# Sigmoid attention and a two-layer MLP on one core: moving operands set 16 floats apart from the weights, and no matmul wider than 448 columns

## Chip, cores and metric

The kernel runs on one core of a Trainium2 chip. The metric is the device time of one execution in microseconds (us); three runs of the kernel before gave 1015.92, 1016.38 and 1016.88 us, with a median of 1016.38 us.

## What is computed

Attention with a sigmoid in place of the softmax, over 8 batches of 12 heads with 448 positions and 64 columns, feeds an MLP of 768 to 2048 to 768 columns over 3584 tokens. All inputs are float32.

```python
scores = scale * np.matmul(q, k.transpose(0, 1, 3, 2)) - np.log(S)
attn = 1.0 / (1.0 + np.exp(-scores))
x = np.matmul(attn, v)                       # then (B*S, 768)
h = x @ w_in
g = h * (1.0 / (1.0 + np.exp(-1.702 * h)))
out = g @ w_out
```

## The kernel before

The program has two stages on TensorE. The first (to about 250 us) is attention: the 48 pairs of heads are taken two at a time, and for each group TensorE runs a burst of score matmuls and then a burst of value matmuls. The second (from 250 us to the end) is the MLP. It is computed by a bilinear scheme with 26 products in place of 32 blocks: weights, x and g are first added up into sums on VectorE, each product is a set of matmuls, and the results are added into the outputs. 104 products of 36 matmuls each make 3744 matmuls.

Precision is kept by splitting. A float32 operand is rounded to the fast float32r form and the rest is kept in a second tile; each product of two operands is three matmuls (hi by hi, hi by rest, rest by hi). `split_pair` (line 628) does this for q and k of a pair of heads into the tile `qk`; `pair_of` (line 1048) does it for x and g into the tile `pair`; `split_piece` (line 827) for the weights into the two ring tiles of the tag `raw64`.

Each matmul has a weight load of its own: 128 columns of the stationary operand (`lhsT`) are loaded, then up to 512 columns of the moving operand (`rhs`) stream past. In the MLP the weights (`w`) are stationary and x or g moves, at line 869. In the scores k is stationary and q moves, at line 673, two matmuls side by side on the two halves of the rows. Both have 448 moving columns of float32r.

Where the operands lie in a partition: every tile of the pools `sb` and `att` has a length that is a multiple of 64 floats (3072 for the weights ring, 1536 for a sum, 3584 for a pair, 1792 for `qk`, 896 for the raw loads and for `a`), and within a tile the slices that a matmul reads begin at multiples of 64 too (448 is 7 times 64, and weights are cut at multiples of 128). So at line 869 and line 673 the stationary and the moving operand begin at the same place, counted mod 64 floats.

The order of all work is worked out ahead by the planner `Plan.run` from fixed costs (line 41 has MM = 0.203 us for a matmul), and each engine runs its list in that order. The change doesn't touch a cost or a task.

`Mlp.products` (line 1091) hands a width to the first matmul of a product that begins a new PSUM accumulator: `self.widths` at line 894, chosen by how many products have passed since the last such one. It replaces the 448 columns of that matmul by 468 to 484. The columns past 448 fall into the unused end of the 512-column PSUM bank, and nothing reads them.

Of the kernel before, what the change touches and what calls it, by code (L numbers as in the profile page):

```python
# [8 lines left out]
F32 = mybir.dt.float32  # L9
F32R = mybir.dt.float32r  # L10
# [9 lines left out]
P = 128  # L20
T = 448
ROWS = 4

PACE, LEAD = 2.9, 1
SOON, PATIENCE, CROWDED, LATE = 4, 0.3, (1, 5), 6.0
# [3 lines left out]
    qk=3, vraw=2, a=6, al=2, raw64=2, e=4, qkraw=5, x32=2,  # L29
# [373 lines left out]
def sigmoid_attention_mlp(ctx: ExitStack, tc: tile.TileContext, qk, v, w, out):  # L403
    nc = tc.nc
    B, HD, S2 = qk.shape
# [3 lines left out]
    S = S2 // 2  # L409
# [15 lines left out]
    sb = ctx.enter_context(tc.tile_pool(name="sb", bufs=2))  # L425
    dram = ctx.enter_context(tc.tile_pool(name="dram", bufs=1, space=bass.MemoryType.DRAM))

    spaces, psum = {}, {}
# [24 lines left out]
    ps = spaces["q0"].tile([P, 512], F32, tag="q0_0", name="still", bufs=1)  # L453
# [149 lines left out]
    def load_pair(b, p):  # L603
# [21 lines left out]
            t_q[0].landing = t_v.landing = LATE if (b, p) <= CROWDED else 3.3  # L625
        return t_q, qkr, t_v, vr

    def split_pair(b, p, t_q, qkr):
        if (b, p) == (0, 0):
            return t_q[0], qkr  # L630
        s = buffer("qk")
        make_s = lambda: make(s, "qk", [P, 2, S2], F32R, f"qk{b}_{p}")
        if (b, p) == (0, 1):
            ts = []
            for t, cols, costs in zip(t_q, (slice(0, S + P), slice(S + P, S2)), ((None, 0.42, 0.72), (None, 0.25, 0.41))):
                ts.append(round_and_rest(
                    costs, s, lambda cols=cols: qkr.tile[:, cols], [t], [qkr],
                    lambda cols=cols: s.tile[:, 0, cols], lambda cols=cols: s.tile[:, 1, cols],
                    lambda: None if s.tile is not None else make_s(),
                ))  # L640
            return ts, s
        t = round_and_rest(
            (0.94, 0.63, 1.09), s, lambda: qkr.tile, t_q, [qkr],
            lambda: s.tile[:, 0], lambda: s.tile[:, 1], make_s,
        )
        return [t], s

# [15 lines left out]
    def scores(n, c, t_s, s, place):  # L663
        ps, a = two_banks(place), buffer("a")

        terms = ((0, 1), (1, 0), (0, 0)) if n else ((0, 0),)

        def emit():
            make(ps, ps.tag, [P, 2, 512], F32, f"sc{n}_{c}")
            src = [s.tile[:, 0], s.tile[:, 1]] if n else [s.tile]  # L670
            for i, (kk, qq) in enumerate(terms):
                for j, rows in enumerate(halves_of_rows):
                    nc.tensor.matmul(  # L673
                        ps.tile[:, j, :S], lhsT=src[kk][rows, S + c * P : S + (c + 1) * P], rhs=src[qq][rows, :S],
                        start=i == 0, stop=i == len(terms) - 1,
                    )

        t = task("PE", (0.8 if not c and n % 2 == 0 else 0.605) if n else (1.2, 1.4, 0.8)[c], emit, t_s, [ps, s])
        return t, sigmoid(f"a{n}_{c}", a, ps, t), a
# [207 lines left out]
    class Mlp:  # L887


        def __init__(self, sequence, before):  # L890
            self.sequence, self.before = sequence, before
            self.w = [Sums(W_SUMS[0], W_USES, w_leaf(m), dve(PIECE), combine, fresh(f"ws{m}", PIECE, "s"),
                           KEEP_FOR[f"w{m}"], self.put_w(m)) for m in range(2)]
            self.gap, self.widths = 1, (0, 472, 484, 476, 468, 472)
            self.saved, self.recent = {}, [(None, None)]
            self.way = self.ways()
            self.x = [Sums(X_SUMS[0], X_USES, self.x_leaf(q), dve(XB), combine, fresh(f"xs{q}", XB, "s"),
                           KEEP_FOR[f"x{q}"], self.put_x(q)) for q in range(2)]
            self.g_nodes = [{}, {}]
            self.g = [Sums(G_SUMS[0], G_USES, self.g_leaf(q), dve(GB), combine, fresh(f"gs{q}", GB, "g"),  # L900
                           KEEP_FOR[f"g{q}"], self.put_g(q)) for q in range(2)]
            self.last_pair = {}
            self.units, self.turn = [], None
            self.nets = {}
            self.products_of = [(q, m, r) for q, m, r in sequence if q < 2]
            for m in range(2):
                for v in W_USES:
                    self.w[m].left[v] -= 1
            for i, (q, m, r) in enumerate(sequence):
                if self.way[i] == "made":  # L910
                    self.w[m].left[W_USES[r]] += 1
                    self.w[m].need(W_USES[r], i)
                if q < 2:
                    (self.x, self.g)[m][q].need((X_USES, G_USES)[m][r], i)
            for q in range(2):
                self.nets[q, 0] = Net(self, q, 0, *H_SUMS, X_SUMS[1], GB, 4, "h", self.gelu)
                self.nets[q, 1] = Net(self, q, 1, *O_SUMS, G_SUMS[1], XB, NJ, "o", self.store)
            self.spilled_g = {}
# [23 lines left out]
        def x_leaf(self, q):  # L942
            def leaf(v):
                k, n = divmod(v, ROWS)
                b = plan.slot()
# [102 lines left out]
        def pair_of(self, q, m, v, n, name, sign):  # L1048
            key = (name, v, sign)
            sums = (self.x, self.g)[m][q]  # L1050
            if key in self.last_pair:
                sums.left[v] -= 1
                sums.used(v)
                return self.last_pair[key]
            node = sums.get(v)
            sums.left[v] -= 1
            b = buffer("pair")
            w = n // T

            def part(d):  # L1060
                return lambda: b.tile[:, d, :w]

            def first():
                make(b, "pair", [P, 2, 4, T], F32R, name)

            if sign > 0:
                t_hi = on_either((act(n), lambda: nc.scalar.copy(part(0)(), node.view())),  # L1067
                                 (cast(n), lambda: nc.vector.tensor_copy(part(0)(), node.view())),
                                 node.done, [b, node.b], first)
            else:  # L1070
                def negative():
                    first()
                    nc.scalar.mul(part(0)(), node.view(), -1.0)

                t_hi = task("ACT", act(n), negative, node.done, [b, node.b])

            def rest():
                if sign > 0:
                    nc.vector.tensor_tensor(part(1)(), node.view(), part(0)().bitcast(F32), op=ALU.subtract)  # L1079
                else:  # L1080
                    nc.vector.scalar_tensor_tensor(
                        part(1)(), node.view(), -1.0, part(0)().bitcast(F32), op0=ALU.mult, op1=ALU.subtract)

            t_lo = task("DVE", dve(n), rest, [t_hi], [b, node.b])
            node.readers += [t_hi, t_lo]
            sums.used(v)
            self.last_pair.clear()
            self.last_pair[key] = t_lo, b
            return t_lo, b
# [253 lines left out]
```

## Time and profile before

| | us |
|---|---|
| median of three runs | 1016.38 |
| span of the profiled execution, first to last instruction | 1014.2 |
| TensorE busy in it | 1009.7 |
| VectorE busy in it | 939.6 |
| ScalarE busy in it | 609.1 |

The profile page gives a span of 1014.2 us for the profiled execution; no whole time of that execution is listed apart. The median of the runs is 2.2 us above the span, which is taken as what lies around it. Busy time is the union of an engine's instructions. Matmuls are pipelined: one lasts about 366 ns from its start to its end, but the next begins some 203 ns after it. So the pace is read from the starts of many matmuls in a row, and not from the mean duration.

### The profile page before, as it was taken

What the parts mean: (1) busy time and instruction counts of PE and PEld (TensorE: products, weight loads), DVE (VectorE), ACT (ScalarE), POOL (GpSimd) and SP (SyncE); (2) the same over time, 40 slices, a digit from 0 to 9 for tenths busy, and PEclk for the clock granted to TensorE, in tenths of its full rate; (3) what the DMA queues carried; (4) which work ended last, traced back from release to release, by engine and by line L of the source; (5) the groups of instructions that cost most, each with busy time, mean ns of one, the idle gap of its engine ahead of it and who ended that gap; (6) DMA issues with size and microseconds to landing.
All of it is one profiled execution on the core that took longest, in us unless ns stands there. A gap on an engine that the chain in (4) does not pass through costs nothing.

```text
span 1014.2 us, 13730 instructions
## 1 busy us (share of the span) xinstructions
PE 1009.7 (100%) x5587; PEld 836.4 (82%) x5587; DVE 939.6 (93%) x658; ACT 609.1 (60%) x489; POOL 0.2 (0%) x4
## 2 busy tenths in 40 slices
PE   9999999999999999999999999999999999999998
PEld 5545555555999999999999999999999999999997
DVE  6987888898899999898999899999999999999996
ACT  7978887895345566356365447675554646344643
POOL 0000000000000000000000000000000000000000
PEclk9999999999999999999999999999999999999999
DMA  9999899777995799968869978996667782889546
GB/s 359 399 384 341 312 383 344 292 257 274 377 365 225 296 346 380 399 253 341 332 242 322 366 275 295 374 393 269 249 244 269 291 324 78 321 327 352 198 151 245
DMA packets 62222, 310.42 MB, mean 306 GB/s; under 512 B 6480, under 2 KB 14928, under 8 KB 58192
## 3 DMA queue, kind: packets, MB, share of 16 engines
q1 hardware_dynamic: 62160, 309.55, 80.6%
q8 instruction: 44, 0.72, 0.3%
q14 instruction: 18, 0.15, 0.0%
HBM read 198.80 MB, written 110.72 MB: 305 GB/s over the span
## 4 chain that ended last, share of the span: by engine, by line
PE 100%; ACT 0%; issue 0%
PE p L869 75%; PE av L704 11%; PE sc L673 9%; PE sc L689 2%; PE av L717 2%; PE still L455 0%; ACT o L1145 0%
## 5 line engine op out<-in xcount | busy, mean ns | idle before, releaser
L869 PE MATMUL p<-gp,w 128*128 128x448 f32 (+2 forms) x1872 | 380.7, 366 | 0.0
L869 PE MATMUL p<-xp,w 128*128 128x448 f32 (+1 forms) x1872 | 380.6, 366 | 0.0
L869 PEld LDWEIGHTS p<-xp,w 128*128 128x128 f32 x1872 | 351.9, 188 | 28.6 <-issue 0.7
L869 PEld LDWEIGHTS p<-gp,w 128*128 128x128 f32 x1872 | 351.9, 188 | 28.2 <-issue 0.2
L659 ACT ACTIVATE a<-sc,bias 128x896 f32<-128x896 f32 x168 | 156.3, 1020 | 37.6 <-PE sc L689 27.5
L1258 ACT COPY h<-p 128x1792 f32<-128x1792 f32 x41 | 67.6, 1658 | 98.0 <-PE p L869 83.7
L704 PE MATMUL av<-a,vraw 128*64 128x448 f32 x576 | 113.5, 543 | 0.1
L1258 ACT COPY o<-p 128x1344 f32<-128x1344 f32 x42 | 53.7, 1283 | 98.8 <-PE p L869 91.2
L673 PEld LDWEIGHTS sc<-qk 64*128 64x128 f32 x846 | 77.1, 185 | 23.7 <-PE sc L689 15.5
L673 PE MATMUL sc<-qk 64*128 64x448 f32 x846 | 92.8, 369 | 0.0
L704 PEld LDWEIGHTS av<-a,vraw 128*64 128x64 f32 x576 | 39.2, 137 | 63.5 <-issue 44.6
L1292 DVE TENSOR_TENSOR h<-h,h 128x1792 f32<-128x1792 f32 x45 | 90.4, 2020 | 0.2
L532 DVE TENSOR_TENSOR qk<-qkraw,qk 128x896 fp32r<-128x896 f32 (+2 forms) x48 | 51.5, 1078 | 3.3 <-ACT qk L526 2.6
L1118 ACT ACTIVATE h<-h 128x1792 f32<-128x1792 f32 x27 | 45.8, 1702 | 11.4 <-DVE h L1292 11.4
L1067 ACT CAST gp<-kg 128x1792 fp32r<-128x1792 f32 x20 | 33.9, 1696 | 28.0 <-DVE kg L810 13.4
L1292 DVE TENSOR_TENSOR o<-o,o 128x1344 f32<-128x1344 f32 x31 | 47.7, 1552 | 0.1
L1079 DVE TENSOR_TENSOR xp<-x,xp 128x1344 fp32r<-128x1344 f32 x28 | 43.5, 1552 | 1.0 <-ACT xp L1067 1.0
L1079 DVE TENSOR_TENSOR gp<-kg,gp 128x1792 fp32r<-128x1792 f32 x21 | 42.4, 2019 | 1.4 <-ACT gp L1067 1.4
L835 DVE TENSOR_TENSOR w<-ws,w 128x1536 fp32r<-128x1536 f32 x23 | 40.3, 1753 | 3.1 <-ACT w L832 2.9
L734 DVE COPY x<-av 128x896 f32<-128x896 f32 x17 | 18.6, 1094 | 23.8 <-PE av L717 23.8
L832 ACT CAST w<-ws 128x1536 fp32r<-128x1536 f32 x17 | 25.2, 1481 | 17.6 <-PE p L869 13.2
L1079 DVE TENSOR_TENSOR gp<-gs,gp 128x1792 fp32r<-128x1792 f32 x17 | 34.4, 2021 | 0.5 <-ACT gp L1067 0.4
(110 smaller groups left out, 930.1 us busy)
## 6 DMA issues: line engine op xcount, KB each, us to landing
kg<-kg SPq DMA_DIRECT2D x34, 896.0 KB, 7.2
w<-w SPq DMA_DIRECT2D x16, 1536.0 KB, 10.2
w<-c SPq DMA_DIRECT2D x32, 768.0 KB, 6.5
c<-w SPq DMA_DIRECT2D x15, 1536.0 KB, 6.9
gl<-g SPq DMA_DIRECT2D x24, 896.0 KB, 7.1
x<-xd SPq DMA_DIRECT2D x31, 672.0 KB, 8.5
qkraw<-qk SPq DMA_DIRECT2D x46, 448.0 KB, 6.1
wf<-f SPq DMA_DIRECT2D x23, 768.0 KB, 7.2
```

What stands on the lines that cost most here:

```text
L532: lambda: nc.vector.tensor_tensor(lo(), src(), hi().bitcast(F32), op=ALU.subtract),
L659: nc.scalar.activation(a.tile, ps.tile[:, :, :S], AF.Sigmoid, bias=bias, scale=scale)
L673: nc.tensor.matmul(ps.tile[:, j, :S], lhsT=src[kk][rows, S + c * P : S + (c + 1) * P], rhs=src[qq][rows, :S], start=i == 0, stop=i == len( ...
L704: nc.tensor.matmul(ps.tile[cols, n % 2, :S], lhsT=vr.tile[:, at : at + D], rhs=a.tile[:, j], start=c == 0, stop=False, skip_group_check=True,)
L832: t_hi = on_either((act(n), lambda: nc.scalar.copy(into()[:, :, 0], src())), (cast(n), lambda: nc.vector.tensor_copy(into()[:, :, 0], src())),
L835: t_lo = task("DVE", dve(n), lambda: nc.vector.tensor_tensor(into()[:, :, 1], src(), into()[:, :, 0].bitcast(F32), op=ALU.subtract), [t_hi ...
L869: nc.tensor.matmul(ps[:, :n], lhsT=ws(c // 6)[:, a, c % 6 * P : (c % 6 + 1) * P], rhs=columns[:, at : at + n], start=start and i == 0 and ...
L1067: t_hi = on_either((act(n), lambda: nc.scalar.copy(part(0)(), node.view())), (cast(n), lambda: nc.vector.tensor_copy(part(0)(), node.view())),
L1079: nc.vector.tensor_tensor(part(1)(), node.view(), part(0)().bitcast(F32), op=ALU.subtract)
L1118: t = task("ACT", act(GB), lambda: nc.scalar.activation(view(), node.view(), AF.Gelu_apprx_sigmoid, scale=float(sign)), [*node.done, *(nod ...
L1258: t = on_either((act(self.n), lambda: nc.scalar.copy(view(), node.view())), (dve(self.n), lambda: nc.vector.tensor_copy(view(), node.view())),
L1292: nc.vector.tensor_tensor(view(), x.view(), y.view(), op=ALU.add if s0 == s else ALU.subtract)
```

## The change

Four things are changed, and no task, cost or order is.

- Before the first `pair` tile is made, a tile of 16 floats named `shift` is allocated in the same pool. Nothing reads or writes it. By the order of allocation x and g, which live in `pair`, then begin 16 floats further on; the weights ring, allocated before, stays.
- The `qk` tile gets gaps. q stays at 0, k goes from 448 to 496 (`GAP` = 48), and the rests go to 960 (`PART`) and 1456. Mod 64, q then begins 16 floats after k. The second pair of heads, which is split in two parts, keeps its old layout without the gap.
- `split_pair` and `scores` follow that layout.
- All entries of `self.widths` are 0, so that each first matmul has 448 columns.

```diff
@@ -20,6 +20,7 @@
 T = 448
 ROWS = 4
+GAP, PART = 48, 960
@@ -625,23 +626,26 @@
+    def apart(s, part):
+        return s.tile[:, part * PART :][:, : 2 * (S + GAP)].rearrange("p (h s) -> p h s", h=2)[:, :, :S]
+
     def split_pair(b, p, t_q, qkr):
...
-        make_s = lambda: make(s, "qk", [P, 2, S2], F32R, f"qk{b}_{p}")
+        make_s = lambda: make(s, "qk", [P, PART + 2 * (S + GAP)], F32R, f"qk{b}_{p}")
...
-                    lambda cols=cols: s.tile[:, 0, cols], lambda cols=cols: s.tile[:, 1, cols],
+                    lambda cols=cols: s.tile[:, cols], lambda cols=cols: s.tile[:, PART:][:, cols],
...
         t = round_and_rest(
-            (0.94, 0.63, 1.09), s, lambda: qkr.tile, t_q, [qkr],
-            lambda: s.tile[:, 0], lambda: s.tile[:, 1], make_s,
+            (0.94, 0.63, 1.09), s, lambda: qkr.tile.rearrange("p (h s) -> p h s", h=2), t_q, [qkr],
+            lambda: apart(s, 0), lambda: apart(s, 1), make_s,
         )
@@ -664,14 +668,15 @@
         terms = ((0, 1), (1, 0), (0, 0)) if n else ((0, 0),)
+        first = S + c * P + (GAP if n > 1 else 0)
...
-            src = [s.tile[:, 0], s.tile[:, 1]] if n else [s.tile]
+            src = [s.tile, s.tile[:, PART:]] if n else [s.tile]
...
-                        ps.tile[:, j, :S], lhsT=src[kk][rows, S + c * P : S + (c + 1) * P], rhs=src[qq][rows, :S],
+                        ps.tile[:, j, :S], lhsT=src[kk][rows, first : first + P], rhs=src[qq][rows, :S],
@@ -891,7 +896,7 @@
-            self.gap, self.widths = 1, (0, 472, 484, 476, 468, 472)
+            self.gap, self.widths = 1, (0, 0, 0, 0, 0, 0)
@@ -1061,6 +1066,8 @@
             def first():
+                if "shifted" not in spaces:
+                    spaces["shifted"] = sb.tile([P, 16], F32, name="shift", tag="shift", bufs=1)
                 make(b, "pair", [P, 2, 4, T], F32R, name)
```

## Rows read from the trace of the kernel before

**Rows 1.** The page: busy time by engine, granted clock in 40 slices, chain by line.

```profile
PE 1009.7 (100%) x5587; PEld 836.4 (82%) x5587; DVE 939.6 (93%) x658; ACT 609.1 (60%) x489; POOL 0.2 (0%) x4
...
PEclk9999999999999999999999999999999999999999
...
PE p L869 75%; PE av L704 11%; PE sc L673 9%; PE sc L689 2%; PE av L717 2%; PE still L455 0%; ACT o L1145 0%
```

**Rows 2.** Waits of TensorE over the span: who for whom, us, times, longest.

```profile
PE still L455 <- PEq L1331: 0.8, 1, 0.8
```

**Rows 3.** Chain in order of time: start us, us, engine, tile, line, count.

```profile
250.47 760.17 PE p L869 x3744
```

**Rows 4.** TensorE, 361 to 388 us: timeline, then by shape with the mean ns.

```profile
360.72 27.52 PE L869 MATMUL p<-xp,w 128*128 128x448 f32 x135
...
L869 PE MATMUL p<-xp,w 128*128 128x448 f32 x135 | 27.5, 365 | 0.0
```

**Rows 5.** Timeline of TensorE, two score bursts: start, length, count.

```profile
36.70 3.98 PE L673 MATMUL sc<-qk 64*128 64x448 f32 x36
...
240.99 3.91 PE L673 MATMUL sc<-qk 64*128 64x448 f32 x36
```

**Rows 6.** All score matmuls of line 673, two records to a pair side by side.

```profile
L673 PE MATMUL sc<-qk 64*128 64x448 f32 x846 | 92.8, 369 | 0.0
```

**Rows 7.** One burst of value matmuls on TensorE's timeline, without its first, and all of line 704.

```profile
245.63 3.93 PE L704 MATMUL av<-a,vraw 128*64 128x448 f32 x20
...
L704 PE MATMUL av<-a,vraw 128*64 128x448 f32 x576 | 113.5, 543 | 0.1
```

**Rows 8.** Weight loads, groups by shape: count, busy us, mean ns, idle before, releaser.

```profile
L869 PEld LDWEIGHTS p<-xp,w 128*128 128x128 f32 x1872 | 351.9, 188 | 28.6 <-issue 0.7
L869 PEld LDWEIGHTS p<-gp,w 128*128 128x128 f32 x1872 | 351.9, 188 | 28.2 <-issue 0.2
```

**Rows 9.** Busy time by stretch, attention's first and last, then the MLP.

```profile
core 0: us, PE busy (x) PEld busy (x) DVE busy (x) ACT busy (x) POOL busy (x), PEclk, DMA share, GB/s
0.00:62.00 62.00, 61.10 (x449) 33.21 (x451) 52.17 (x60) 53.74 (x56) 0.20 (x4) 1.00 0.97 377
...
188.00:250.00 62.00, 62.00 (x468) 32.96 (x464) 51.57 (x49) 48.66 (x50) 0.00 (x0) 1.00 0.75 278
250.00:350.00 100.00, 100.00 (x499) 92.26 (x492) 95.17 (x65) 46.16 (x31) 0.00 (x0) 1.00 0.80 306
350.00:450.00 100.00, 100.00 (x494) 92.63 (x493) 95.23 (x62) 54.18 (x37) 0.00 (x0) 1.00 0.96 370
450.00:550.00 100.00, 100.00 (x494) 92.66 (x494) 96.01 (x60) 53.77 (x37) 0.00 (x0) 1.00 0.76 287
550.00:650.00 100.00, 100.00 (x495) 92.64 (x494) 93.03 (x56) 58.24 (x38) 0.00 (x0) 1.00 0.88 329
650.00:750.00 100.00, 100.00 (x495) 92.64 (x494) 99.82 (x56) 59.72 (x42) 0.00 (x0) 1.00 0.79 306
750.00:850.00 100.00, 100.00 (x494) 92.65 (x493) 98.20 (x58) 51.34 (x38) 0.00 (x0) 1.00 0.68 253
850.00:950.00 100.00, 100.00 (x493) 92.39 (x493) 97.74 (x58) 50.21 (x36) 0.00 (x0) 1.00 0.75 287
950.00:1010.00 60.00, 60.00 (x297) 55.62 (x297) 54.27 (x33) 26.91 (x22) 0.00 (x0) 1.00 0.55 199
```

**Rows 10.** MLP matmuls of 472 and 484 columns, by shape: count, busy us, mean ns.

```profile
L869 PE MATMUL p<-xp,w 128*128 128x472 f32 x29 | 11.0, 380 | 0.0
L869 PE MATMUL p<-gp,w 128*128 128x472 f32 x19 | 7.2, 377 | 0.0
L869 PE MATMUL p<-gp,w 128*128 128x484 f32 x12 | 4.5, 378 | 0.0
L869 PE MATMUL p<-xp,w 128*128 128x484 f32 x7 | 2.6, 378 | 0.0
```

**Rows 11.** Splitting q and k, on VectorE: count, ns min/median/max, first and last start.

```profile
L527 DVE CAST qk<-qkraw x38: 618/627/674, 8.5 to 233.0; 128x896 fp32r<-128x896 f32 x38
```

## The prediction

> **What bounds the kernel now.** I read the page first. TensorE is busy for 1009.7 of the 1014.2 us of the span, at a granted clock of nine tenths or more in all 40 slices, which is the 2.4 GHz level throughout [rows 1]. The chain that ended last lies wholly on TensorE, 75% of it on line 869 and 9% on line 673 [rows 1]. TensorE's list of waits holds one entry, 0.8 us at the start [rows 2]. So no engine and no transfer makes TensorE wait; the time is the number of matmuls times their pace, and the question is what sets the pace.
>
> The pace comes from starts. The MLP is one unbroken piece of 760.17 us with 3744 matmuls [rows 3], 203.0 ns each. A stretch with 448 columns only gives it more cleanly: 135 records span 27.52 us [rows 4]; less 0.365 us, the length of one record, 27.155 us over 134 intervals are 202.6 ns. At 2.4 GHz 448 columns need 448/2.4 = 186.7 ns. So each matmul pays 16 ns over its columns.
>
> Two other rows show that this is not a fixed fee. Of a burst of value matmuls, 20 records, ten pairs, span 3.93 us, and a record lasts 0.543 us [rows 7], so a pair takes (3.93 - 0.543)/9 = 0.376 us. These float32 matmuls stream their 448 columns at half the rate, two records in 373.3 ns, so they pay about 3 ns. And of two score bursts with the same 18 pairs, one lasts 3.91 us and the other 3.98 us [rows 5]. The 0.07 us lie on some 17 intervals, 4.1 ns each: same shapes, same addresses mod 64, but 206.8 instead of 202.6 ns. The fee is small when the moving stream runs at half speed, and at full speed it has two values at least. That is how a collision between two streams looks, here the moving operand and the weights loaded for the next matmul, whose outcome depends on how they stand to each other. That it is a collision is inferred; no row names it.
>
> **Against the skill.** The Trainium skill says otherwise: "TensorE: Matmul & The Clock Gate" (Step-by-step, LDWEIGHTS) and "SBUF — State Buffer" (Who interferes with whom) give TensorE two independent read ports and say that loading the next weights takes nothing from the running matmul. By that rule the addresses change nothing, and only the narrower matmuls are left. The two paces [rows 5] speak against it, but don't disprove it: that rule is the second rival below.
>
> **The change, part by part.**
>
> *The offset in the MLP.* It adds no instruction. `shift` is only allocated. It moves x and g from 0 to 16 floats past the weights, mod 64, for all 3744 matmuls. The trace of before has no matmul at another offset, so the price is bounded from both sides. The good end is the fee of the value matmuls, 3 ns, a pace of 189.5 ns. The weight loads forbid little more: one lasts 188 ns, with 28.6 + 28.2 us idle between 3744 of them [rows 8], so that a pace much under 190 ns would have to wait for them. The bad end is the slower burst, 206.8 ns. Between 189.5 and 206.8 I take 196: about half of the 13 ns between the pace now and the good end. The reason is that 16 floats part the two streams at the start, but the moving one runs faster, goes through its 64 floats in 64 columns, and so must come upon the weight stream again while that is being read. Some of the fee should go and some stay. This is an estimate, and it is the softest number here.
>
> *What the other engines let through.* At 196 ns the same matmuls take 196/202.6 = 96.7% of their time. No cost of the planner changes, so every engine keeps its list. VectorE is next: in the seven stretches of 100 us from 250 to 950 us it is busy for 95.17, 95.23, 96.01, 93.03, 99.82, 98.20 and 97.74, and for 54.27 of the last 60 [rows 9]. In the first four TensorE at 96.7 remains the longer, 386.8 us together. In the next three VectorE does: its busy time is 295.8 us, and if its few idle times there are waits of its own it stays at 300; I take 298. The last 60 become 58. The MLP then takes 386.8 + 298 + 58 = 742.8 in place of 760 us, a gain of 17.2 us where the pace alone would give 24.7. ScalarE is at 60% at most, and the DMA share is 0.55 to 0.96 [rows 9], so neither comes first.
>
> *The offset in the scores.* Line 673 has 846 records, 423 pairs [rows 6]; the 9 pairs of the second pair of heads keep the old layout, so 414 change. At 6.6 ns each that is 2.7 us. It counts in full only if attention's transfers keep up: the DMA share is 0.97 in the first 62 us and 0.75 in the last [rows 9]. I keep 2.7; the low end is 0.
>
> *The narrower matmuls.* 67 of 472 and 484 columns stand in the rows [rows 10], and there are four more of 468 and 476. Their 24, 36, 20 and 28 extra columns at 2.4 GHz are 10, 15, 8.3 and 11.7 ns: 48 x 10 + 19 x 15 + 2 x 8.3 + 2 x 11.7 = 805 ns, all on the chain. In the stretches where VectorE leads it is hidden, so 0.5 us.
>
> *The gaps and the split.* Rounding and resting write two runs of 448 instead of one of 896, the same 896 elements: 627 ns on VectorE [rows 11], or the same copy on ScalarE. I cost them at nothing; should a second run cost 0.05 us, 46 pairs of heads with two operations each make 4.6 us on VectorE, which is idle 10 of the last 62 us of attention [rows 9], so it hides. No wait, DMA or queue entry is added or moved.
>
> **Sum.** 17.2 + 2.7 + 0.5 = 20.4 us. The span 1014.2 becomes 993.8; with the 2.2 us around it, 996.0 us, against the median of 1016.38.
>
> The ends of this case: at 189.5 ns (93.5% of the time) TensorE leads in one of the first four stretches, 95.2 + 95.2 + 96.0 + 93.5; VectorE's 295.8 and 56.1 for the last give 731.8, a gain of 28.2 us, and the scores give 5.4: 982.5 us. At 200.5 ns (99%) it is 396 + 299 + 59.4 = 754.4, a gain of 5.6, with 0.9 and 0.6 more: 1009 us. So 983 to 1009.
>
> **Rivals.**
>
> *The streams collide more often, or the paces change places.* The slow burst [rows 5] shows that 206.8 ns is a pace on which TensorE can stay for a whole burst. A new offset might make it the rule; and the wide first matmuls may be what keeps the MLP off it, since they shift the streams in time, and they are taken away. Against the second reason stands the stretch of 135 matmuls without one [rows 4]: it passes three starts of products and keeps 202.6. Price: 4.1 ns x 3744 = 15.4, and 4.1 x 414 less the few slow bursts already there, 1.4 us, less 0.8 for the columns: 16 us, 1032 us. From a pace of 203.4 ns on (3 us more for 3744, less 0.8) the change is slower by over 0.2%. VectorE hides none of it.
>
> *The offset changes nothing.* The fee is a fixed cost of full-rate streaming with a weight load beside it, or the allocator puts `shift` behind `pair` and x and g don't move. Then only the columns go: 1016.38 - 0.8 = 1015.6 us. For it: 202.6 ns holds almost everywhere, whatever the tile. Against it: the two paces at equal shapes [rows 5]. The rule of the Trainium skill named above would have it so.
>
> *The fee goes and VectorE takes over.* This is the good end of the forecast, 982.5 us; I count it there.
>
> **How the numbers follow.** The forecast's case has 0.70, the offset without effect 0.13, the slower pace 0.17. Within 0.2% (2.0 us, about what a measurement of this kernel can tell) lies the second rival, so faster 0.70, same 0.13, slower 0.17. The predicted time is that of the forecast, 996 us. The range runs from the good end, 983, over the case without effect to 1017, and leaves out the slower pace.
>
> **What would show it.** In the profile after, an unbroken run of matmuls at line 869 should have starts 190 to 200 ns apart, and likewise the pairs at line 673; a pace of 202.6 says that the offset does nothing, 206 that the collision is worse. The shapes of 472 and 484 columns should be gone. VectorE should be at 98% or more of the MLP's stretches, and TensorE should show waits for it, which it now has none of; if the pace falls and such waits don't appear, my limit by VectorE was too strict and the time lies lower. The value matmuls should keep 376 ns for a pair, since their operands move together. The forecast is wrong if the pace at line 869 is above 202 ns or the MLP's stretch is not shorter than 755 us.

## The result and the profile after

The changed kernel takes 1008.16 us (median of four executions, 1006.96 to 1008.70), the kernel before, run beside it, 1016.31 us (1015.92 to 1016.88). The ratio is 0.9918, with a 95% interval from 0.9904 to 0.9932: faster by 8.2 us. The prediction had the direction right, and its wide range (983 to 1017 us) holds the time, but it forecast a gain of 20.4 us: more than half of that didn't come.

The page of the changed kernel, the lines that answer to [rows 1]: busy time by engine, the chain by engine, the chain by line.

```profile
PE 1000.3 (99%) x5587; PEld 833.1 (83%) x5587; DVE 938.6 (93%) x658; ACT 610.0 (61%) x489; POOL 0.2 (0%) x4
...
PE 80%; DVE 14%; issue 4%; ACT 1%; DMA 1%; DVEq 0%; ACTq 0%
PE p L874 55%; PE av L709 11%; PE sc L678 9%; DVE gp L1086 3%; DVE h L1299 2%; PE sc L694 2%; PE av L722 2%; DVE w L840 2%; DVE gl L815 1%; DVE xp L1086 1%; DVE kg L815 1%; DVE o L1299 1%; DVE gs L815 1%; DMA wf<-f 1%; DVE x L815 0%
```

The chain was wholly TensorE's before; now 14% of it is VectorE's. (The MLP's matmuls stood on line 869 and stand on 874; other lines moved by one to seven.) TensorE's busy time fell by 9.4 us, VectorE's work is the same to 1 us. TensorE's list of waits, which held one entry before [rows 2], now reads:

```profile
PE p L874 <- DVE w L840: 1.1, 1, 1.1
PE still L456 <- PEq L1338: 0.8, 1, 0.8
PE p L874 <- DVE gp L1086: 0.5, 2, 0.3
PE p L874 <- ACT h L1265: 0.4, 1, 0.4
```

The pace comes from a stretch without a wait, as it did in [rows 4]: start, length and count of a piece of TensorE's timeline near 361 us.

```profile
360.78 27.56 PE L874 MATMUL p<-xp,w 128*128 128x448 f32 x137
```

Less the 0.362 us of one record, 27.20 us over 136 intervals are 200.0 ns, where 202.6 ns stood. Read from the starts of all records, every product of the MLP runs at 200.0 ns. The MLP is no longer one piece [rows 3]: the starts show 20 gaps between 408 and 955 us, 4.4 us together, and the chain leaves TensorE and returns to it after them. Two of its pieces (start, length, count), and the timeline at the largest gap, 1.47 us from one matmul's start to the next one's:

```profile
249.93 237.90 PE p L874 x1188
...
748.78 116.12 PE p L874 x578
```

```profile
744.71 2.96 PE L874 MATMUL p<-gp,w 128*128 128x448 f32 x14
748.78 2.44 PE L874 MATMUL p<-gp,w 128*128 128x448 f32 x11 [1.11 <-DVE w L840]
```

Busy time by stretch, to be held against [rows 9]; the columns are length, then TensorE, weight loads, VectorE, ScalarE and GpSimd, then granted clock, DMA share and GB/s.

```profile
550.00:650.00 100.00, 99.62 (x499) 93.03 (x498) 94.04 (x57) 57.88 (x38) 0.00 (x0) 1.00 0.88 329
650.00:750.00 100.00, 98.89 (x495) 92.38 (x494) 99.87 (x56) 60.78 (x44) 0.00 (x0) 1.00 0.75 286
750.00:850.00 100.00, 100.00 (x501) 93.26 (x500) 98.51 (x59) 52.73 (x38) 0.00 (x0) 1.00 0.70 260
850.00:950.00 100.00, 99.71 (x494) 91.92 (x493) 97.65 (x57) 49.41 (x35) 0.00 (x0) 1.00 0.78 293
950.00:1004.00 54.00, 53.11 (x265) 49.09 (x263) 48.18 (x30) 23.32 (x20) 0.00 (x0) 1.00 0.55 203
```

The largest gap falls where VectorE is busiest, from 650 to 750 us, at an unchanged granted clock. (Busy time runs to the modelled end of the last matmul, so it hides most of the shorter gaps; of the 4.4 us, read from the starts, 1.4 us lie in that stretch and 1.5 us between 850 and 950 us.)

So the bill of the MLP is short. From first to last start it took 759.9 us and takes 753.2. 3744 matmuls at 203.0 ns (the 202.6 and the wide ones) became 3744 at 200.0: 11 us less. The gaps give 4.4 us back. With the half microsecond by which the MLP starts earlier (it starts between 249.9 and 252.4 us in the profiles of kernels with the same attention code, so this is no gain), that is the 7.3 us by which the span is shorter (1014.2 to 1006.9).

Attention gave next to nothing (0.1 us from its first burst of line 678 to its last), though its pace fell too. The last score burst and the value burst behind it, of before (its first line is in [rows 5]) and of after; PEld is the weight load, with what released it.

```profile
244.82 0.20 PEld L704 LDWEIGHTS av<-a,vraw 128*64 128x64 f32 x4 [0.30 <-ACT a L659]
```

```profile
240.45 3.90 PE L678 MATMUL sc<-qk 64*128 64x448 f32 x36
241.43 5.50 ACT L663 ACTIVATE a<-sc,bias 128x896 f32<-128x896 f32 x6 [0.58 <-PE sc L678]
244.29 0.20 PEld L709 LDWEIGHTS av<-a,vraw 128*64 128x64 f32 x4 [0.32 <-ACT a L663]
244.29 4.73 PE L709 MATMUL av<-a,vraw 128*64 128x448 f32 x24
```

The value burst begins 3.84 us after the score burst in the changed kernel (240.45 to 244.29), and it began 3.84 us after it before (240.99 to 244.83). Its weight load is released by ScalarE's sigmoid in both: it begins 51 to 56 ns after the third sigmoid of the burst ends, and that is 3.78 us after the burst's start in both, since the first sigmoid starts 0.98 us after it and the next two follow without a break. Inside the burst the pairs start 200 to 202 ns apart where they had 202.6; the last pair stands 309 ns before the value matmuls, where it stood 290. What the pairs gain, that wait takes.

### The profile page after: what moved, and what is told of

Its sections match the earlier page's. It is cut to its first block, busy times and chain, and to the rows that moved or that the text cites. A ratio compares the mean times of both kernels' runs of the same rounds, so it can differ in the third digit from the quotient of the medians.

```text
span 1006.9 us, 13730 instructions
## 1 busy us (share of the span) xinstructions
PE 1000.3 (99%) x5587; PEld 833.1 (83%) x5587; DVE 938.6 (93%) x658; ACT 610.0 (61%) x489; POOL 0.2 (0%) x4
## 4 chain that ended last, share of the span: by engine, by line
PE 80%; DVE 14%; issue 4%; ACT 1%; DMA 1%; DVEq 0%; ACTq 0%
PE p L874 55%; PE av L709 11%; PE sc L678 9%; DVE gp L1086 3%; DVE h L1299 2%; PE sc L694 2%; PE av L722 2%; DVE w L840 2%; DVE gl L815 1%; DVE xp L1086 1%; DVE kg L815 1%; DVE o L1299 1%; DVE gs L815 1%; DMA wf<-f 1%; DVE x L815 0%
## 5 line engine op out<-in xcount | busy, mean ns | idle before, releaser
L874 PE MATMUL p<-gp,w 128*128 128x448 f32 x1872 | 377.2, 362 | 1.7 <-DVE w L840 1.1
L874 PE MATMUL p<-xp,w 128*128 128x448 f32 x1872 | 375.4, 362 | 0.4 <-ACT h L1265 0.4
```

The source lines that it names most:

```text
L874: nc.tensor.matmul(ps[:, :n], lhsT=ws(c // 6)[:, a, c % 6 * P : (c % 6 + 1) * P], rhs=columns[:, at : at + n], start=start and i == 0 and ...
```

## The experiments

**The price of each distance.** The tile of x and g was given room for 64 floats more, and each pair of x or g its own start (102 pairs for the 104 products), so that one kernel shows many distances; the score tiles likewise.

```diff
+X_AHEAD = [4 * (i % 16) for i in range(64)] + [0, 1, 2, 3, 14, 15, 16, 17, 18, 19, 30, 31, ...] * 3
...
-                make(b, "pair", [P, 2, 4, T], F32R, name)
+                make(b, "pair", [P, 8 * T + 64], F32R, name)
+                b.tile = b.tile[:, ahead : ahead + 8 * T].rearrange("p (d k t) -> p d k t", d=2, k=4)
```

> The changed kernel, but the distance of the moving operand from the weights (mod 64 floats) differs from burst to burst and from product to product: 0 to 60 in steps of 4, and some odd ones. All operands lie at most 64 floats elsewhere; the result is computed in full. Theory A, a collision of the two streams in places that repeat every 64 floats: the pace at line 869's matmuls and in the score bursts depends on the distance, with 202.7 ns at 0 and 200.0 ns at 16, and other distances lie on both sides of these, by several ns. Theory B, the streaming fee is fixed and the distance only picks between locked paces: every distance gives one of 200.0, 202.7 and 206.7 ns. Theory C, the fee doesn't depend on the distance at all and the 2.7 ns came with the wide matmuls that are gone: 200.0 ns everywhere, at 0 too.

> The scan of distances again, with the 32 distances that the first scan left out in the MLP. If 200.0 ns is a floor that no distance goes below: several at 200.0, the others up to 213. If the whole fee depends on the distance: some distance at 187 to 198 ns.

1019.29 us, and 1020.45 us for the second kernel, with the distances that the first left out. The time of these two means nothing, the pace of each product does, read from the starts of its 36 matmuls. Here are 37 of the 64 distances:

```
floats from weights to x or g, mod 64          ns from start to start, settled
3 7 10 15 16 19 27 31 35 40 42 47 51 59 63     200.0 in every product
34, 62                                         200.0 too, after up to eight slower starts
0                                              202.7
12, 20, 48                                     203.0, 203.3, 202.3
32, 44, 8                                      203.9, 204.2, 204.6 or 206.7
2, 17, 18, 28, 30, 36, 46, 50                  206.7 to 206.8
41, 1, 33                                      208.9, 206.7 or 210.0, 213.3
```

So the distance matters, by up to 13 ns, and it repeats: a distance has the same pace wherever its product stands, but for a few that have two (1, 4, 8 and 55 among them). 16 floats is one of seventeen best ones. At 0 the scan gives the pace of the kernel before and at 16 that of the changed kernel, so `shift` did move x and g. And no distance goes below 200.0 ns: 13.3 ns over the 186.7 ns of streaming stay at all 64. The prediction's good end, 189.5 ns, is at no distance.

The table is that of the MLP, where x and g move and the weights stay at a multiple of 64. In the scores it is the stationary operand, k, that moves, and the pace changes there too, from 200 to 211 ns; so the place of the moving operand alone doesn't make it. But the numbers are others: 28 floats give 200.0 there and 206.7 in the MLP, 31 floats 206.7 there and 200.0 in the MLP. Almost all score bursts start 10.2 to 10.3 us apart all the same.

**The wide matmuls alone.** The kernel before with 448 columns throughout.

```diff
-            self.gap, self.widths = 1, (0, 472, 484, 476, 468, 472)
+            self.gap, self.widths = 1, (0, 0, 0, 0, 0, 0)
```

> The kernel before with its widths set to 0 and nothing else. If the wide matmuls only cost their columns (my prediction): 0.8 us less, 1015.5 us, pace 202.7 ns throughout. If they hold the MLP off the slow pace: some products at 206.7 ns, up to 15 us more, 1017 to 1031 us. If they themselves cost the 2.7 ns (theory C): 200.0 ns and 1008 us.

1015.23 us (1014.24 to 1019.51), ratio 0.9999 [0.9988, 1.001]: nothing gained, and a scatter of 5 us where the kernel before has 1. The timeline of this kernel, a stretch at 622 us and one near the end:

```profile
622.39 14.75 PE L869 MATMUL p<-xp,w 128*128 128x448 f32 x72
...
959.69 51.62 PE L869 MATMUL p<-gp,w 128*128 128x448 f32 x249
```

(14.75 - 0.365)/71 = 202.6 ns, and (51.62 - 0.365)/248 = 206.7 ns. The starts show where it turns: behind a gap of 268 ns at 906.9 us, and the last 13 products stay at 206.7. The kernel before has a gap of 251 ns at 908.0 us, and there the pace stays. It turns at the next wide matmul, of 484 columns, at 915.4 us, and turns back at the one behind it, of 472 columns, at 922.8 us; the stretches behind the gap and behind each of the two, in the kernel before:

```profile
908.29 6.64 PE L869 MATMUL p<-gp,w 128*128 128x448 f32 x32
...
915.81 6.78 PE L869 MATMUL p<-gp,w 128*128 128x448 f32 x32
...
923.05 6.64 PE L869 MATMUL p<-gp,w 128*128 128x448 f32 x32
```

Less 0.365 us, over 31 intervals, these are 202.4, 206.9 and 202.4 ns (the starts of the three products settle at 202.7, 206.7 and 202.7). So at distance 0 there are two paces. A gap can tip TensorE from one to the other, and a wide matmul can tip it either way: one of the 19 with 484 columns did, the first behind the gap, and the next wide one undid it. Without wide matmuls nothing took the pace back in the one execution with a profile: 13 products at 4 ns a matmul cost 1.9 us against 0.8 us of columns saved. That the extra columns keep slow stretches short, and so the scatter at 1 us, fits with this, but rests on that one case. Six of the ten executions took 1014.2 to 1015.5 us, where the kernel before, beside them, took 1015.4 to 1016.7; four took 1016.6 to 1019.5. The first may be those in which the pace didn't tip; one of the four is the one with the profile.

**The wide matmuls in the changed kernel.** The same line, the other way round.

> The changed kernel with the old widths of 468 to 484 columns put back. If at 16 floats the pace is one and the same whatever came before, the wide matmuls only cost columns: 0.8 us of TensorE's work, of which the part before waits for VectorE hides, so 1008.2 to 1009.0 us. If they shift the pace there too: a pace of another value than 200.0 ns in some products, over 1010 us.

1008.45 us (1007.98 to 1008.86), ratio 0.9926 [0.9909, 0.9942]: no different from the changed kernel. At 16 floats the pace of the changed kernel is 200.0 ns again after each of the 20 gaps, without any wide matmul, so there is nothing for them to mend. The gaps are fewer here, 6 with 1.9 us; the extra columns probably fill some of the time in which TensorE waits for VectorE.

**Another distance of the same pace.** 40 floats in place of 16.

```diff
-GAP, PART = 48, 960
+GAP, PART = 24, 960
...
-                    spaces["shifted"] = sb.tile([P, 16], F32, name="shift", tag="shift", bufs=1)
+                    spaces["shifted"] = sb.tile([P, 40], F32, name="shift", tag="shift", bufs=1)
```

> The changed kernel with x, g and q 40 floats ahead of the weights in place of 16 (a tile of 40 floats ahead of the pair tiles, a gap of 24 in the scores). The first scan has 200.0 ns at both, at 40 with every interval 200. If the pace is all that counts: 1007.5 to 1008.8 us. If the steady interval helps at the starts of products: up to 1 us less.

Two executions took 1007.51 and 1009.16 us (ratio 0.9923 [0.9903, 0.9943]), two 1025.09 and 1029.76 us; the profile is that of 1025.09. TensorE's timeline in it, ahead of 410 us and later:

```profile
299.70 20.56 PE L874 MATMUL p<-xp,w 128*128 128x448 f32 x102
...
699.70 40.46 PE L874 MATMUL p<-gp,w 128*128 128x448 f32 x195
```

(20.56 - 0.363)/101 = 200.0 ns, then (40.46 - 0.365)/194 = 206.7 ns, at a granted clock of 1.00 in all of it. A gap of 276 ns at 409.9 us lies between, and the pace doesn't come back: some 2950 matmuls at 6.7 ns are the 20 us. (A gap of 286 ns at 279.8 us in the same execution had left the pace at 200.0 ns, so a gap can tip it and need not.) So equal paces in a scan don't make distances equal. At 16 floats no gap in any profile here tipped the pace. That the fourth execution was tipped in the same way, earlier, is inferred from its time; it has no profile.

**The score gaps taken away.** The kernel before, with the tile of 16 floats and the narrower matmuls only.

```diff
-            self.gap, self.widths = 1, (0, 472, 484, 476, 468, 472)
+            self.gap, self.widths = 1, (0, 0, 0, 0, 0, 0)
...
+                if "shifted" not in spaces:
+                    spaces["shifted"] = sb.tile([P, 16], F32, name="shift", tag="shift", bufs=1)
```

> The kernel before with one tile of 16 floats put ahead of the products' buffers, so that x and g begin 16 floats further on, and with no wider matmuls; the score tiles and their operands stay where they were. If the shift is all of the gain, it takes the time of the changed kernel, 1008.2 us (1007.0 to 1008.7). If the score gaps bring part of it, it is later by up to 2.7 us, the prediction's term: 1009 to 1011 us. If the gaps cost something, it is earlier.

1007.55 us (1007.24 to 1008.01), ratio 0.9915 [0.9900, 0.9930]. That is the whole gain without the gaps in the score tiles: 2.7 us were predicted for them, and none are there.

**VectorE's work cut.** Half of the columns of the in-place additions to h and o are left out; all waits and tasks stay.

```diff
+            if held_as == "own":
+                def emit(op=ALU.add if s0 == s else ALU.subtract):
+                    part = [f()[:, :, : T // 2] for f in (view, x.view, y.view)]
+                    nc.vector.tensor_tensor(*part, op=op)
```

> The changed kernel, but VectorE's in-place additions into the hidden and output accumulators work on the first half of the columns only (the other half of each sum is left out). That takes some 60 us off VectorE's 938, all in the MLP; the order of all lists stays. If VectorE's amount of work makes the gaps between matmuls from 550 to 955 us: the gaps of 4.4 us go, MLP 749 us, 1003 to 1005 us. If the gaps are waits for transfers or ScalarE: they stay, 1007 to 1009 us.

1004.89 us (1004.45 to 1005.54), ratio 0.9888 [0.9871, 0.9904]. The same stretches as above:

```profile
550.00:650.00 100.00, 100.00 (x502) 93.75 (x501) 79.61 (x56) 55.73 (x37) 0.00 (x0) 1.00 0.88 336
650.00:750.00 100.00, 100.00 (x502) 93.75 (x501) 93.20 (x56) 60.59 (x44) 0.00 (x0) 1.00 0.75 291
750.00:850.00 100.00, 100.00 (x502) 93.75 (x501) 90.43 (x59) 53.49 (x39) 0.00 (x0) 1.00 0.69 256
```

TensorE idles no more: two gaps with 0.3 us are left and 0.1 us behind the MLP's first matmul, and the MLP takes 749.0 us, which is 3743 intervals of 200.0 ns and these. VectorE is busy for 655 us from 250 us on, where it was 728. So the gaps come of VectorE's amount of work, and 1004.9 us is what the pace of 200.0 ns gives without them.

**VectorE's work moved.** Copies and splits that the planner put on VectorE in the MLP are written out for ScalarE when that comes free at the latest 0.2 us after (five tasks), or 0.6 us after (seventeen).

```diff
...
-            t.emits[e]()
+            if e == "DVE" and "ACT" in t.costs and when > 245 and max(free["ACT"], moved) <= when + 0.2:
+                moved = max(free["ACT"], moved, when) + t.costs["ACT"]
+                t.emits["ACT"]()
+            else:
+                t.emits[e]()
```

> The changed kernel with five copies and splits, placed by the planner on VectorE in the MLP, written out for ScalarE instead where ScalarE was to come free at the latest 0.2 us after; nothing else is moved. If the 4.4 us of gaps are VectorE's amount of work, five times some 1.3 us of it less takes away part of them: 1005 to 1007.5 us. If a moved task makes another wait on ScalarE that TensorE sees, no change or slower: 1008 to 1010 us.

> As the run before it, with seventeen of these tasks written out for ScalarE (where it was to come free within 0.6 us after), some 22 us of VectorE's work. If VectorE's amount of work is the cause of the gaps and ScalarE, busy 610 of 1007 us, takes it without being late, the gaps go and the time is that of the run with half of the additions left out, 1004.9 us; if the moved tasks hold up ScalarE's evictions, its waits come in place of VectorE's and the time is 1008 us or more.

1008.23 us (1007.99 to 1008.45), ratio 0.9921 [0.9906, 0.9936], and 1008.59 us (1007.92 to 1009.63), ratio 0.9923 [0.9906, 0.9939]: no gain from either. One stretch of the first kernel, two of the second, and the timeline of the first at the gap:

```profile
650.00:750.00 100.00, 98.90 (x495) 92.38 (x494) 99.87 (x57) 60.77 (x43) 0.00 (x0) 1.00 0.76 291
```

```profile
650.00:750.00 100.00, 100.00 (x499) 92.80 (x497) 99.87 (x56) 60.69 (x43) 0.00 (x0) 1.00 0.77 295
750.00:850.00 100.00, 98.63 (x494) 92.46 (x494) 98.16 (x57) 57.18 (x41) 0.00 (x0) 1.00 0.70 260
```

```profile
739.74 9.16 PE L878 MATMUL p<-gp,w 128*128 128x448 f32 x45
750.01 10.24 PE L878 MATMUL p<-gp,w 128*128 128x448 f32 x50 [1.11 <-DVE w L844]
```

VectorE's busy time falls by 4.9 and 13.8 us. The tasks went from where ScalarE had room, mostly before 650 us. From 650 to 750 VectorE is as full as it was, and the largest gap is still there, 1.47 and 1.73 us. Of all gaps 1.9 and 2.8 us are left, against 4.4; but the kernel with the shift alone, whose MLP is planned alike, shows 2.9 in its profile, so a microsecond or two of gaps isn't told apart from chance, and the times show none of it. These runs say where the work must not be taken from, not that a better move doesn't exist.

**A planner that knows the pace.** The planner's price of a matmul is set to what was measured.

```diff
-ISSUE, LANDING, PER_KB, MM = 0.43, (2.2, 3.0), 0.0027, 0.203
+ISSUE, LANDING, PER_KB, MM = 0.43, (2.2, 3.0), 0.0027, 0.200
...
-        t = task("PE", (0.8 if not c and n % 2 == 0 else 0.605) if n else (1.2, 1.4, 0.8)[c], emit, t_s, [ps, s])
+        t = task("PE", (0.8 if not c and n % 2 == 0 else 0.6) if n else (1.2, 1.4, 0.8)[c], emit, t_s, [ps, s])
```

> The changed kernel with the planner told 0.200 us for a matmul (it was 0.203) and 0.600 for three score pairs (0.605). The trace after has 20 gaps between matmuls of the MLP, 4.4 us together, that before had not. If they come from a list that was ordered for the slower pace: fewer gaps, 1004 to 1006 us. If VectorE's amount of work between 650 and 950 us is what ends first: the same 4 us of gaps, 1007 to 1010 us.

1040.79 us (1038.94 to 1041.81), ratio 1.0241 [1.0226, 1.0256]: slower than the kernel before. TensorE's list of waits, its first four, and two stretches of it:

```profile
PE p L874 <- issue: 8.2, 1, 8.2
PE p L874 <- DVE w L840: 6.7, 2, 6.3
PE p L874 <- ACT h L1265: 5.1, 1, 5.1
PE p L874 <- ACT p L1222: 4.0, 1, 4.0
```

```profile
450.00:550.00 100.00, 86.71 (x412) 80.22 (x411) 89.11 (x55) 49.55 (x33) 0.00 (x0) 0.91 0.69 263
550.00:650.00 100.00, 100.00 (x502) 93.73 (x501) 88.37 (x57) 48.85 (x33) 0.00 (x0) 1.00 0.81 290
```

The planner, which replaces every later choice when one price moves, made another order, in which four waits take 4 to 8 us each. After each of the four, eight to eleven matmuls start 373 to 374 ns apart, which is 448 columns at 1.2 GHz; over the first stretch shown, with one of the waits and the start of another, the granted clock is 0.91. The truer price gave the worse plan; why this order has such waits wasn't followed up.

**Whose fee it is.** Bursts of 24 equal matmuls ahead of the kernel's own work, on one tile. First of the rounded 4-byte type that the MLP and the scores use (float32r), with other widths and fewer weight columns:

```diff
...
+    for name, columns, n, ahead in PROBES:
+        ps = spaces["q0"].tile([P, 512], F32, tag="q0_0", name=name, bufs=1)
+        for i in range(24):
+            nc.tensor.matmul(ps[:columns, :n], lhsT=probe[:, :columns], rhs=probe[:, ahead : ahead + n], start=i == 0, stop=i == 23)
```

> The changed kernel with twelve bursts of 24 float32r matmuls ahead of everything, on a tile of constants: 448, 512, 384 and 256 moving columns with 128 columns of weights at a distance of 16 floats; 64 and 32 columns of weights with 448 moving ones at 16; 128 and 64 columns of weights at 0 and at 33; 512 columns at 33. No distance of the first scan gave less than 200.0 ns, so 13.3 ns over the 186.7 ns of 448 columns stay. Theory A, the rest of the fee is the weight load's share of the reads: 13.3 ns with 128 columns of weights, 6.7 with 64, 3.3 with 32, the same 13.3 at 512, 384 and 256 moving columns (226.7, 173.3, 120.0 ns). Theory B, the chain of weight loads sets the floor (187 ns and some 13 until the matmul begins): 200 ns at 384 and 256 columns too, 213 to 216 at 512, and less with fewer columns of weights. Theory C, a fee of float32r streaming itself, whatever the weights: 13.3 ns with 64 and 32 columns of weights, in proportion to the moving columns (215 + 13 at 512).

Then the same in other types, by a view of the tile as bfloat16 or plain float32:

> Bursts of 24 equal matmuls on one tile, put ahead of the kernel's own work, so their own time is added to the kernel's. The question is to whom the 13.3 ns belong that a matmul of 448 moving columns takes over its streaming at the best distances (200.0 against 186.7 ns). If they are a matter of the 4-byte type (a row of 448 floats is 1792 bytes a partition, twice that of bfloat16), a burst in bfloat16 is less than 200 ns apart, near 187 to 193 ns. If they belong to every matmul of this size, bfloat16 shows 200 ns too, or the 202 to 213 ns of the poorer distances. A burst in plain float32 (four passes for one product) is expected at 4 times the streaming, about 747 ns, plus one fee of 13 ns if the fee is of the instruction and four if it is of the pass, about 800 ns. Bursts with 32 weight columns at distances 0 and 33 and with 320 moving columns at 33 and 16: if the part of the fee that hangs on the distance comes of the weight load reading its columns while the moving operand is read, 32 weight columns (loaded in 108 ns) narrow the difference between distance 0 and 33, which was 202.5 against 210.9 ns with 128; if it hangs on the alignment alone, the difference stays about 8 ns.

The bursts on the timelines of the two kernels (1067.74 and 1087.79 us with them): start, length, name, count.

```profile
9.07 5.79 PE L468 MATMUL wide<-probe 128*128 128x512 f32 x24
14.92 4.44 PE L468 MATMUL narrow<-probe 128*128 128x384 f32 x24
19.41 3.09 PE L468 MATMUL short<-probe 128*128 128x256 f32 x24
...
43.17 5.32 PE L468 MATMUL bad<-probe 128*128 128x448 f32 x24
```

```profile
9.24 4.70 PE L469 MATMUL bfloat<-probe 128*128 128x448 bf16 x24
14.00 4.70 PE L469 MATMUL bfloatzero<-probe 128*128 128x448 bf16 x24
18.76 18.31 PE L469 MATMUL plain<-probe 128*128 128x448 f32 x48
37.12 18.31 PE L469 MATMUL plainzero<-probe 128*128 128x448 f32 x48
...
60.88 5.07 PE L469 MATMUL faster<-probe 128*128 128x448 f32 x24
```

The first few starts of a burst stand further apart. The mean behind the first four intervals, from the starts:

```
type, weight columns, moving columns   distance   ns apart   over streaming
float32r 128, 448                      16, 51     200.0      13.3
float32r 128, 512 / 384 / 320 / 256    16         228.7 / 173.4 / 146.6 / 117.8   15.4 / 13.4 / 13.3 / 11.1
float32r 128, 448                      0, 33      202.5, 210.9
float32r 128, 320                      33         148.9
float32r  64, 448                      16, 0, 33  201.4, 202.5, 209.7
float32r  32, 448                      16, 0, 33  206.6, 202.1, 206.6
bfloat16 128, 448                      0, 16      189.2      2.5
bfloat16 128, 512                      16         215.8      2.5
float32 128, 448, each of two records  0, 16      375.8      2.5
```

(At 33 with 128 weight columns the mean hides two paces: some 208 ns first, 213 over the last eleven, which is the MLP's pace at 33.) Of these forms, only float32r at full rate pays the fee of 13.3 ns. bfloat16 streams the same columns at the same rate beside its own weight loads, and pays 2.5 ns at either distance. Plain float32 gives two records to a product, each at half the rate, and a record pays 2.5 ns at either distance too. By their sizes both read half as many bytes in a ns as float32r does, 896 bytes a partition in 186.7 ns or 1792 in 373.3, against 1792 in 186.7; so the bursts don't tell the type from the rate in bytes. In float32r the fee doesn't shrink with the weights (from 128 to 64 columns it is 13.3 and 14.7 ns), so a lighter weight load doesn't remove it; it isn't the weight loads' own chain either, which at 188 ns each couldn't let 256 columns go at 117.8; and it grows only from 11 to 15 ns while the columns double. Fewer weight columns do change what a distance costs (33 against 0 is 8.4 ns with 128, 4.5 with 32, and 16 is then no better than 33), so that part hangs on both operands. What makes the remaining 13 ns of float32r stays open.

## Why the prediction was right or wrong

**What bounds the kernel: right.** TensorE's pace did, and the time moved with it. The granted clock is 1.00 in every stretch of the MLP, before and after. No wait in TensorE's list names a transfer; one of 8.5 us, the weights `wf`, stands in the chain that ended last, ahead of the gap at 908 us.

**The offset in the MLP: the direction right, the size wrong, and this is the step that failed.** It took 196 ns as the middle between 202.6 and a good end of 189.5 ns, and the good end was the fee of the value matmuls [rows 7]. That row doesn't bear on this. The prediction read the small fee of the half column rate as what a matmul at the full rate could come down to by its addresses; the value matmuls are plain float32, the MLP's are float32r, and float32r has a floor of 200.0 ns at all 64 distances. (The half column rate by itself isn't what makes the fee small: the burst in bfloat16 has the small fee at the full one. The type may do it, or the bytes read in a ns.) So of the 16 ns that a matmul paid, 2.7 were the distance's and 13.3 were not, and the change could take the 2.7 at best, and took them. That these 2.7 ns are a collision of two streams is still only inferred: the runs show that the pace hangs on the distance and on the weight columns, and no row names the cause. The second support of the good end, that weight loads of 188 ns forbid a pace much under 190 ns [rows 8], doesn't hold either: in the burst with 256 moving columns the loads last 188 ns and the matmuls start 117.8 ns apart. The doubt named beside the number, that some of the fee would stay, was right; the half was not read from anything. Nor was the poor end of the case, 200.5 ns and 1009 us, which came within 1 us of the result: that is luck. (The slow pace of the two bursts, 202.6 + 4.1, is 206.7 ns and not 206.8; nothing hangs on it.)

**What the other engines let through: right.** TensorE waits for VectorE as forecast, and the run with half of the additions left out shows that it is VectorE's amount of work. VectorE isn't at 98% in all stretches, as the prediction had asked, but at 94.0 to 99.9% up to 950 us: at 200.0 ns it is the longer engine in a short piece only. The prediction's own sum carries it: with 200.0 in place of 196 the four first stretches are 4 x 98.7 = 394.9, the three next 298 and the last 59.2, together 752.1, a gain of 8.1 us of the 760.2; measured 753.2. With 0.5 for the columns and none for the scores that is 1007.8 us, and 1008.16 came.

**The offset in the scores: wrong, 2.7 us predicted and none found.** The pace fell as said. But the prediction looked for a cover in the transfers alone, and it is ScalarE: a value burst waits for a sigmoid that ends 3.8 us after the score burst began, at either pace. [rows 5] shows only what a slower pace costs (3.98 against 3.91 us), not what a faster one saves. The row to look at was the weight load of the value matmuls, which in the kernel before names ScalarE as its releaser.

**The narrower matmuls.** The 0.8 us of columns were counted rightly, but the columns can also do something: one tipped the pace into the slow one and the next took it back. Taken alone the edit gains nothing (0.9999). The prediction named the loss of the wide matmuls as a reason for a slow pace and held the 135 matmuls of [rows 4] against it; these have no gap among them, and in the run without wide matmuls the pace tipped behind a gap. It cost nothing in the changed kernel, where 16 floats showed only one pace.

**The gaps, the split, the value matmuls: as costed.** VectorE is busy for 938.6 us after 939.6, and the value matmuls are those of [rows 7]:

```profile
L709 PE MATMUL av<-a,vraw 128*64 128x448 f32 x576 | 113.5, 543 | 0.1
```

**The rivals.** The slower pace didn't come, but it was near: 206.7 ns is the pace of some twenty of the 64 distances, and of 40 floats after a gap. The rival in which the offset changes nothing was wrong for the 2.7 ns and right for the 13.3: those stay at every distance, as that rival had it for the whole fee. The rule that the prediction set beside it, of the Trainium skill, "TensorE: Matmul & The Clock Gate" (Step-by-step, LDWEIGHTS), is that loading the next weights takes no read bandwidth from the running matmul. The bursts in bfloat16, equal at both distances, agree; the float32r matmuls of the MLP, from 200.0 to 213.3 ns by the distance alone, speak against it, though no row names the reading as what collides. The same page of the Trainium skill (Wait — 56ns, not 53.3ns?) gives a warm matmul its columns at 2.4 GHz and some 2.5 ns, and a cold one exactly its columns at 1.2 GHz. The traces agree for bfloat16 (189.2 and 215.8 ns), for each record of plain float32 (375.8 ns, 2.5 ns over 448 columns at half the rate) and for the half clock (373 to 374 ns); for float32r at the full clock they show 13.3 ns in its place.

## What to carry to other kernels

Take the good end of a price from a row of the same operand type and rate, or measure it in a burst of two dozen matmuls first: a row that differs in both doesn't say which of the two makes its fee. Before a faster pace is counted in a stage, look at what releases the first instruction behind the burst; where it is another engine in a fixed time after the burst's start, only a slower pace will show. And where the pace of matmuls depends on how two operands lie, choose a placement whose pace the profiles show to be the same after a wait, not only one that is fast as long as nothing waits.

## What the runs showed of the hardware

- In the MLP a float32r matmul with 128 weight and 448 moving columns starts 200.0 to 213.3 ns after the one before, by the distance of its operands mod 64 floats, and on average over a product never less than 200.0; a bfloat16 one of a burst starts 189.2 ns after.
- One distance can have two paces, each held over hundreds of matmuls or thousands: 202.7 and 206.7 ns at 0, 200.0 and 206.7 ns at 40 floats. Gaps of 268 ns (at 0) and 276 ns (at 40 floats) tipped it, gaps of 251 and 286 ns did not; at 0 a matmul of 36 columns more tipped it once and one of 24 more took it back.
- At the half clock the fee isn't there: float32r matmuls of 448 columns start 373 to 374 ns apart, which is their streaming alone.
- Four waits of 4.4 to 8.6 us, from one matmul's start to the next one's, were each followed by a stretch at 1.2 GHz; the 20 gaps of the changed kernel, 1.5 us at most, were not.
